# Loading a float64 weight's words into idle buffers, splitting the first key and query loads over two queues, and a newly derived order of work

## The chip, the cores and the metric

The kernel runs on one core of one Trainium2 chip. The metric is the device time of one execution in microseconds, as the median over runs. The engines named below are PE (TensorE), DVE (VectorE), ACT (ScalarE), POOL (GpSimd) and SP (SyncE, which here only issues DMAs).

## The reference

Three layers follow one another on x of 4 batches x 576 positions x 512 features.

1. Attention with 8 heads of 64: scores = q k^T / 8; in each row the 32nd largest score is the threshold, all below it are dropped, and a softmax over the rest weighs v.
2. A channel mix: xk and xr are blends of x and x shifted by one position; k = relu(xk w_k); v = (k*k) w_v; r = sigmoid(xr w_r); the result is r * v. w_k is 512 x 1024, w_v 1024 x 512, w_r 512 x 512, and all three arrive as float64.
3. A mixture of 8 experts: each token goes to one expert (the argmax of a gate, or the expert of the token before it where a local gate says so), and out = p[e] * (relu(x w1[e]) w2[e]).

## The kernel before, in words

The tokens are 18 tiles of 128. Attention goes tile by tile and, within a tile, over four pairs of heads: 72 pairs. One pair does: score matmuls (L511 for batch 0, L516 for the other batches), eviction by ACT (L498), 16 chunk maxima on DVE (MAX8, L534), candidates (L544, L547), a count (L566), a mask on POOL (L571), the threshold (L575, L578), relu on ACT (L581), subtraction on POOL (L585), exp (L589), transposes on PE (L612) and the product with v (L625). Layer 2 (`moe`, matmuls L823, L888, L916) runs for two tiles at a time beside the attention of later tiles. Then the tokens are sorted by expert and layer 3 runs.

PE takes float32 weights as a high and a low part, so `narrow` turns each 128 x 512 block of a float64 weight from pairs of 32-bit words into those two parts. There are 20 blocks, called in the order w_k (8), w_r (4), w_v (8). The steps of one block, by line: load of the raw words (L735, 512 KB); `o1` on ACT (L696); `o1b`, `o2`, `o3`, `o4` on DVE (L699, L702, L705, L708); `o4b` on ACT (L711); `hi_` on ACT (L722); a product on POOL (L719); `sum_` on PE (L725 to L727); `lo_` on ACT (L730). The raw words lie in a buffer of tag `rw` (2 buffers), the integer result of `o3` in tag `xf` (1 buffer), which `o3` takes and `sum_` and `hi_` read. The results for w_v lie in tag `wv` (8 buffers, each 128 x 2 x 512).

`Sched` sets the order before the program is built. It takes each operation with a duration, its dependencies and its buffers, plays the engines forward in a model of time, and at each free engine starts the ready operation with the lowest priority number. That number is the one in the call plus `SHIFT` of the operation's kind, plus its running index times `SLOPE`. Buffers of one tag are handed out in the order of their creation. The resulting order of start is the order in which instructions are issued; on the chip each engine takes its own list strictly in order, so an instruction that waits holds all behind it. A load in the model lands 2.3 us after its issue step ends, whatever else is under way.

`keys(b, hp)` loads the keys of two heads with four DMAs into `kn` (1 buffer), two for each head; the transposes (L391) wait for all four. `queries(t)` loads one tile of q into `qn` (1 buffer). `small` loads four small tensors (L1270 to L1273). All of these are issued on SP. `fill` puts matmuls that compute nothing (L1856) into PE's gaps in the early part of the plan.

Of the kernel before, what the change touches and what calls it, by code (L numbers as in the profile page):

```python
# [146 lines left out]
def kernel(  # L147
# [48 lines left out]
    def segs(t):  # L196
        r = []
        g = t * P
        while g < (t + 1) * P:
# [40 lines left out]
    SHIFT = {"ACT Routing.own.<lambda>": 1600.4, "ACT keys.hi": -8273.1, "ACT mix.o1": -201.7, "ACT mix.o3": -55.0,  # L240
             "ACT moe.ev": -9550.0, "ACT moe.hi": -95.1, "ACT moe.rc": 2604.1, "ACT moe.rl": -1080.6,
             "ACT moe.sig": 9217.2, "ACT moe.sq": -2233.7, "ACT narrow.hi_": -6878.4, "ACT narrow.lo_": -3354.4,
             "ACT narrow.o1": -12605.5, "ACT narrow.o4b": 7243.4, "ACT narrow.o8": 82.5, "ACT pair.<lambda>": -3944.7,
             "ACT pair.cnt": 213.0, "ACT pair.cp": 153.5, "ACT pair.ev": -1356.5, "ACT pair.ex": 943.6,
             "ACT pair.ex2": 235.0, "ACT pair.nm": 645.5, "ACT pair.rl": -2339.7, "ACT queries.hi": -1850.3,
             "ACT slots.fin": -1800.3, "ACT slots.rl": 1990.9, "ACT slots.thi": -2317.5, "ACT slots.xhi": -8276.7,
             "ACT split.hi": 4421.4, "ACT x0_t.cs": -8538.1, "ACT x0_t.ev": -41.7,
             "DVE Routing.__init__.<lambda>": -8985.9, "DVE Routing.own.<lambda>": -2828.9,
             "DVE Routing.place.<lambda>": 1634.7, "DVE Routing.place.counts": -7047.9,
             "DVE Routing.place.order": 5600.6, "DVE Routing.place.rows": 2003.5, "DVE keys.lo": -172.9,  # L250
             "DVE mix.o1": 544.4, "DVE mix.o2": -1964.2, "DVE moe.lc": -7257.5, "DVE moe.lo": 12.5,
             "DVE moe.xs": 162.4, "DVE narrow.o1b": -1351.0, "DVE narrow.o2": 483.8, "DVE narrow.o3": 375.2,
             "DVE narrow.o4": -257.8, "DVE narrow.o9": 203.0, "DVE pair.cands": 3976.7, "DVE pair.ch": -3687.6,
             "DVE pair.cn": -78.5, "DVE pair.nm": -41.5, "DVE pair.r1": -646.5, "DVE pair.rx": -109.0,
             "DVE pair.th": -290.3, "DVE queries.lo": 1224.6, "DVE slots.tlo": 1053.5, "DVE slots.xlo": -1378.6,
             "DVE split.hi": 5962.0, "DVE split.lo": -1691.1, "DVE kernel.nmu": -4805.2,
             "DVE kernel.ok_in": 1377.0,
             "DVE kernel.ok_out": -2597.9, "DVE x0_t.nrm": -3136.3,
# [6 lines left out]
             "POOL Routing.place.<lambda>": 5051.1, "POOL Routing.pool.consts_": -4153.1, "POOL mix.o1": 921.0,  # L265
             "POOL mix.o4": 110.0, "POOL moe.lo": 4123.7, "POOL moe.sq": -133.5, "POOL narrow.o5": 8398.3,
             "POOL narrow.o5r": -256.8, "POOL narrow.o6": -5082.6, "POOL narrow.o9": -14.0, "POOL pair.nbias": 3171.8,
             "POOL pair.rp": 446.6, "POOL pair.sp": -4172.9, "POOL slots.gx": 794.9, "POOL slots.sca": 6498.8,
             "POOL slots.tlo": -5777.7, "POOL split.lo": -834.2, "POOL x0_t.edge": 1874.6, "SP dma.go": 763.5,
             "SP dma.keys": 1140.5, "SP dma.kspread": 10261.3, "SP dma.qspread": -8740.8, "SP dma.queries": 686.5,  # L270
             "SP dma.raw": -11550.7, "SP dma.small": 912.7, "SP dma.vals": 3870.3, "SP load.go": -7105.4,
             "SP moe.<lambda>": -2208.6}
    SLOPE = {"ACT Routing.own.<lambda>": -861.9774, "ACT keys.hi": -45.9238, "ACT mix.o1": 16.4916,
             "ACT moe.ev": -27.2409, "ACT moe.hi": 1.4502, "ACT moe.rc": -108.553, "ACT moe.rl": 14.1884,
             "ACT moe.sig": -3.9868, "ACT moe.sq": 20.7524, "ACT narrow.hi_": 87.4735, "ACT narrow.lo_": 165.5799,
             "ACT narrow.o1": -35.4432, "ACT narrow.o4b": 78.6359, "ACT pair.<lambda>": 1.236, "ACT pair.ev": -1.9141,
             "ACT pair.ex": 2.3394, "ACT pair.rl": 0.1234, "ACT queries.hi": -79.7598, "ACT slots.fin": -42.3376,
# [1650 lines left out]
```

## Time and profile before

| | us |
|---|---|
| median of 3 runs | 1061.44 |
| lowest and highest of these | 1056.66, 1063.55 |
| the profiled execution, its own time | 1057.62 |
| its span, first to last instruction | 1055.8 |

Busy time in the span: PE 988.2, DVE 880.2, ACT 778.6, POOL 754.4. The profile is one execution; PE's busy time includes the fill matmuls. A wait is put down to what came last before the waiting instruction began.

### The profile page before, as it was taken

To read this page: it belongs to the slowest core of one execution; us is meant where nothing else is said; L and a number is where in the kernel's file an instruction comes from. 1 tells how busy PE (TensorE), PEld (TensorE's weight loads), DVE (VectorE), ACT (ScalarE), POOL (GpSimd) and SP (SyncE) were. 2 spreads that over 40 slices of the span, in tenths; PEclk is the share of its full clock that TensorE was granted. 3 is DMA by queue.
4 is the path that set the end of the run, shared out by engine and by line. 5 is a ranking of instruction groups with operands and counts; after the bars stand their busy time and mean duration, and the time that the engine had idled before them with its cause. 6 is when DMAs were issued, how large, how long until landed. Compare 5 with 4: busy or idle time off the path is not lost.

```text
span 1055.8 us, 24502 instructions
## 1 busy us (share of the span) xinstructions
PE 988.2 (94%) x7790; PEld 827.2 (78%) x7790; DVE 880.2 (83%) x3589; ACT 778.6 (74%) x1763; POOL 754.4 (71%) x858
## 2 busy tenths in 40 slices
PE   7898998899999999999999999999859999999896
PEld 6687884678787788888888788877759889888784
DVE  4998997858999999999989999958695669777672
ACT  4776786976999989989989799885335566566452
POOL 2686986666898989989978899873356757566552
PEclk9999999999999999999999999999789999999898
DMA  7421123234212353221342211003813646666650
GB/s 182 123 56 54 54 62 96 62 82 104 61 44 70 93 132 81 49 66 37 91 103 70 66 42 41 22 1 112 287 51 116 226 150 230 217 206 202 207 182 19
DMA packets 100974, 109.49 MB, mean 104 GB/s; under 512 B 49374, under 2 KB 67806, under 8 KB 100832
## 3 DMA queue, kind: packets, MB, share of 16 engines
q1 hardware_dynamic: 97312, 97.32, 32.4%
q0 software_dynamic: 3520, 10.49, 2.9%
q8 instruction: 64, 1.05, 0.4%
q14 instruction: 78, 0.64, 0.2%
HBM read 76.57 MB, written 10.49 MB: 82 GB/s over the span
## 4 chain that ended last, share of the span: by engine, by line
PE 58%; DVE 21%; ACT 8%; DMA 6%; issue 4%; SPq 0%; POOL 0%; POOLq 0%; DVEq 0%; ACTq 0%
PE pv L1808 9%; PE pb L1758 9%; PE xa L625 6%; PE pv L916 5%; PE pb L888 5%; PE pb L612 5%; DVE c L534 4%; PE pb L516 4%; PE pb L823 3%; DVE c L575 2%; PE pb L1768 2%; DVE mk L566 2%; PE pb L511 2%; PE pv L1856 2%; DMA rw<-in_moe_w_k_dram 2%
## 5 line engine op out<-in xcount | busy, mean ns | idle before, releaser
L585 POOL TENSOR_TENSOR at<-s,at 128x576 f32<-128x576 f32 x144 | 205.0, 1435 | 31.0 <-ACT at L581 30.4
L571 POOL TENSOR_TENSOR mk<-s,mk 128x576 f32<-128x576 f32 x144 | 205.6, 1428 | 0.0
L534 DVE MAX8 c<-s 128x8 f32<-128x72 f32 x1152 | 166.5, 219 | 4.8 <-ACT s L498 4.8
L581 ACT ACTIVATE at<-s,TS 128x576 f32<-128x576 f32 x144 | 112.1, 783 | 16.2 <-DVE TS L578 15.8
L1758 PE MATMUL pb<-xk,wk 128*128 128x256 f32 x864 | 114.6, 289 | 7.2 <-DVE xk L1740 7.2
L1758 PEld LDWEIGHTS pb<-xk,wk 128*128 128x128 f32 x864 | 112.3, 196 | 10.7 <-DVE xk L1740 7.5
L575 DVE MAX8 c<-mk 128x8 f32<-128x584 f32 x144 | 108.4, 757 | 14.6 <-POOL mk L571 14.6
L589 ACT ACTIVATE at<-at,sm 128x576 f32<-128x576 f32 x144 | 113.0, 786 | 7.7 <-POOL at L585 7.3
L498 ACT ACTIVATE s<-pb 128x288 f32<-128x288 f32 (+1 forms) x320 | 110.1, 418 | 8.4 <-PE pb L516 4.5
L612 PE MATMUL pb<-ident,at 128*128 128x128 f32 x648 | 99.1, 281 | 17.0 <-ACT at L589 11.8
L566 DVE TENSOR_SCALAR_CACHE_REDUCE mk<-s,c 128x576 f32<-128x576 f32 x144 | 114.8, 801 | 0.0
L615 ACT ACTIVATE aT<-pb 128x384 f32<-128x384 f32 x216 | 98.5, 497 | 12.7 <-PE pb L612 12.1
L916 PE MATMUL pv<-wv,kk 128*128 128x512 f32 x384 | 106.5, 406 | 0.0
L888 PE MATMUL pb<-xk,wk 128*128 128x256 f32 x768 | 103.9, 286 | 0.0
L612 PEld LDWEIGHTS pb<-ident,at 128*128 128x128 f32 x648 | 74.0, 142 | 37.5 <-ACT at L589 17.7
L625 PE MATMUL xa<-aT,vb 128*64 128x128 f32 (+1 forms) x1600 | 98.6, 269 | 2.4 <-ACT aT L615 1.8
L888 PEld LDWEIGHTS pb<-xk,wk 128*128 128x128 f32 x768 | 95.2, 188 | 2.9 <-issue 1.4
L625 PEld LDWEIGHTS xa<-aT,vb 128*64 128x64 f32 x1600 | 80.8, 138 | 19.2 <-issue 11.1
L1808 PE MATMUL pv<-wv,vb 128*128 128x512 f32 x330 | 88.5, 402 | 0.9 <-ACT xT L1816 0.9
L516 PE MATMUL pb<-kT,qx 128*128 128x288 f32 x480 | 86.5, 314 | 1.4 <-DMA kT<-rw 0.8
L1702 DVE TENSOR_TENSOR wk<-s,wk 128x512 fp32r<-128x512 f32 x67 | 70.7, 1088 | 16.1 <-ACT wk L1699 8.9
L516 PEld LDWEIGHTS pb<-kT,qx 128*128 128x128 f32 x480 | 69.6, 188 | 13.3 <-issue 5.3
(258 smaller groups left out, 2232.1 us busy)
## 6 DMA issues: line engine op xcount, KB each, us to landing
s<-in_moe_w_dram SPq DMA_DIRECT2D x88, 256.0 KB, 4.1
kT<-in_moe_w_dram SPq DMA_DIRECT2D x44, 512.0 KB, 5.1
qx<-qh SPq DMA_DIRECT2D x112, 64.0 KB, 2.0
qx<-ql SPq DMA_DIRECT2D x112, 64.0 KB, 2.0
kT<-rw SPq DMA_DIRECT2D x48, 144.0 KB, 2.6
xd<-rr SPq DMA_DIRECT2D x18, 256.0 KB, 2.2
rw<-in_moe_w_k_dram SPq DMA_DIRECT2D x8, 512.0 KB, 4.8
qn<-in_q_dram SPq DMA_DIRECT2D x16, 256.0 KB, 3.1
```

What stands on the lines that cost most here:

```text
L516: nc.tensor.matmul(dst(hf), qx.t[:, w, a, hp % 2, :], kt.t[:, a, c], start=(w == 0), stop=(w == 1))
L534: nc.vector.max(c8.t[:, a, c, :], s2.t[:, c * CH:(c + 1) * CH])
L566: nc.vector.tensor_scalar(mk.t[:, :S], s2.t, c8.t[:, a, NCH + 2, 7:8], 0.0, op0=OP.is_lt, op1=OP.add, accum_out=sm.t[:, 2 + a:3 + a])
L571: nc.gpsimd.tensor_tensor(mk.t[:, :S], s2.t, mk.t[:, :S], op=OP.mult)
L575: nc.vector.max(c8.t[:, a, 0, :], mk.t)
L585: nc.gpsimd.tensor_tensor(x, s2.t, x, op=OP.subtract)
L612: nc.tensor.transpose(pt.t[:, c * P:(c + 1) * P], at.t[:, (g * GB + c) * P:(g * GB + c + 1) * P], ident)
L625: nc.tensor.matmul(xa.t[a * D:(a + 1) * D, hp * P + p0:hp * P + p0 + n], vb[:, a, j, :], evs[c // GB][1].t[:, c % GB, p0:p0 + n], start=(j ...
L888: nc.tensor.matmul(pm.t[:, :N], WK[c][f // 4].t[:, x, f % 4 * P:(f % 4 + 1) * P], xk.t[:, y, c, :N], start=(m == 0), stop=(m == 3 * DC - 1))
L916: nc.tensor.matmul(pvs[ti].t, kk.t[:, x, ti * P:(ti + 1) * P], WV[f].t[:, y, :], start=(f == 0 and m == 0), stop=(f == FB - 1 and m == 2))
L1758: nc.tensor.matmul(ph.t[:, (f % 2) * N:(f % 2 + 1) * N], w[:, x], xt.t[:, y, c, :], start=(n == 0), stop=(n == 3 * DC - 1))
L1808: nc.tensor.matmul(py.t, hT.t[:, x, o_:o_ + P], w[0].t[:, y, :], start=(f == 0 and m == 0), stop=(f == FC - 1 and m == 2))
```

## The change

Raw words of w_k go to buffers of tag `wv` (`RAWK`, eight of them, created ahead of `WV`) and no longer to `rw`; w_r and w_v still use `rw`. Their load has a kind of its own, `rawk`. The model's landing time of all raw loads is 4.0 us, where it was 2.3 us. The second head's half of the very first key load, and the query load of tile 0, are issued on ACT's DMA queue; everything else stays on SP's. All of `SHIFT` and `SLOPE` have new values, and with them the whole order is derived again; the durations of the model stay.

```diff
-    SHIFT = {...  "SP dma.keys": 1140.5, "SP dma.kspread": 10261.3, "SP dma.qspread": -8740.8, "SP dma.queries": 686.5,
-             "SP dma.raw": -11550.7, "SP dma.small": 912.7, "SP dma.vals": 3870.3, ...
+    SHIFT = {...  "SP dma.keys": 934.8, "SP dma.kspread": 13318.2, "SP dma.qspread": -14480.5, "SP dma.queries": 1855.7,
+             "SP dma.raw": -14362.7, "SP dma.rawk": -223.3, "SP dma.small": 1776.8, "SP dma.vals": 1851.8,
...
-    SLOPE = {...  "SP dma.keys": 14.5103, "SP dma.raw": 27.5676, ...
+    SLOPE = {...  "SP dma.keys": 63.7004, "SP dma.raw": 10.391, "SP dma.rawk": 65.9593, ...
...
     WK = [[new("wk", [P, 2, 512], F32R) for _ in range(2)] for _ in range(DC)]
+
+    RAWK = [new("wv", [P, 2, DM]) for _ in range(2 * DC)]
     WV = [new("wv", [P, 2, DM], F32R) for _ in range(FB)]
...
         def go():
-            x, e, kk_ = kn.t, nc.sync, k[b, 2 * hp:2 * hp + 2]
+            x, kk_ = kn.t, k[b, 2 * hp:2 * hp + 2]
             for h in range(2):
+
+                e = nc.scalar if h and not (b or hp) else nc.sync
                 e.dma_start(x[:REM, :, h, :], kk_[h, :cut].rearrange("(p j) d -> p j d", j=KJ + 1))
                 e.dma_start(x[REM:, :KJ, h, :], kk_[h, cut:].rearrange("(p j) d -> p j d", j=KJ))
...
-                nc.sync.dma_start(qn.t[p0:p0 + n], q[b, :, s:s + n, :].rearrange("h p d -> p h d"))
+                (nc.sync if t else nc.scalar).dma_start(qn.t[p0:p0 + n], q[b, :, s:s + n, :].rearrange("h p d -> p h d"))
...
     def narrow(dst, split, c, f0, src, prio, lod=False):
         n = 512
-        raw = new("rw", [P, 2, S])
+        far = src is w_k
+        raw = RAWK[2 * c + f0 // n] if far else new("rw", [P, 2, S])
...
-        ld = dma([...], 1.5, prio - PAR['ra'], [raw], kind="raw")
+        ld = dma([...], 1.5, prio - PAR['ra'], [raw], kind="rawk" if far else "raw")
+        ld.lat = 4.0
```

## Rows read from the trace of the kernel before

**Rows 1.** The page: span, busy time by engine, DVE in 40 slices (tenths).

```profile
span 1055.8 us, 24502 instructions
PE 988.2 (94%) x7790; PEld 827.2 (78%) x7790; DVE 880.2 (83%) x3589; ACT 778.6 (74%) x1763; POOL 754.4 (71%) x858
DVE  4998997858999999999989999958695669777672
```

**Rows 2.** Busy time by stretch: us, then each engine (instructions), clock, DMA share, GB/s.

```profile
0.00:22.30 22.30, 16.68 (x189) 14.36 (x190) 8.15 (x20) 9.75 (x18) 4.16 (x14) 1.00 0.69 172
22.30:110.00 87.70, 80.41 (x878) 66.89 (x877) 80.63 (x357) 62.10 (x140) 62.04 (x69) 0.94 0.30 82
110.00:200.00 90.00, 82.00 (x748) 61.33 (x746) 81.20 (x355) 71.00 (x152) 71.22 (x72) 0.96 0.26 70
200.00:715.00 515.00, 499.23 (x4136) 415.42 (x4137) 470.63 (x2412) 457.36 (x1100) 436.30 (x540) 1.00 0.27 66
715.00:800.00 85.00, 69.00 (x402) 58.21 (x401) 65.48 (x214) 32.71 (x64) 33.14 (x35) 0.84 0.47 157
```

**Rows 3.** Chain that ended last, 0 to 110 us: shares by line.

```profile
by line: DMA rw<-in_moe_w_k_dram 17.3%; PE pb L511 8.4%; PE pv L1856 8.1%; DMA qn<-in_q_dram 5.3%; DVE xf L705 5.0%; DVE c L575 5.0%; DVE c L534 4.9%; PE pb L612 4.4%; DVE mk L566 4.2%; DMA rw<-in_moe_w_r_dram 3.8%; PE xa L625 3.4%; PE pb L
```

**Rows 4.** Instructions in order of time, 0 to 24 us: start, duration, engine, line.

```profile
0.75 0.89 SPq L735 DMA_DIRECT2D rw<-in_moe_w_k_dram  x2
...
4.66 0.67 ACT L696 ACTIVATE xT<-rw 128x512 f32<-128x512 f32 x1 [2.63 <-DMA rw<-in_moe_w_k_dram]
...
6.00 0.66 ACT L696 ACTIVATE xT<-rw 128x512 f32<-128x512 f32 x1 [0.67 <-DMA rw<-in_moe_w_k_dram]
...
9.32 0.67 SPq L377 DMA_DIRECT2D kn<-in_k_dram  x1
...
16.27 0.63 PE L391 MATMUL pb<-ident,kn 128*128 128x128 f32 x4 [2.39 <-DMA kn<-in_k_dram]
...
19.14 0.53 PE L511 MATMUL pb<-kT,qh 64*128 64x288 f32 x2
...
20.35 0.67 ACT L696 ACTIVATE xT<-rw 128x512 f32<-128x512 f32 x1 [2.70 <-DMA rw<-in_moe_w_k_dram]
...
21.92 1.30 ACT L498 ACTIVATE s<-pb 128x288 f32<-128x288 f32 x4
...
22.35 2.25 DVE L534 MAX8 c<-s 128x8 f32<-128x72 f32 x16 [0.21 <-ACT s L498]
```

**Rows 5.** DMA issues of 0 to 3 us: size of one, median us to landing.

```profile
rw<-in_moe_w_k_dram SPq DMA_DIRECT2D x2, 512.0 KB, 4.3
qn<-in_q_dram SPq DMA_DIRECT2D x1, 256.0 KB, 5.8
```

**Rows 6.** DMA issues of 9.2 to 12 us, the first keys, columns as above.

```profile
kn<-in_k_dram SPq DMA_DIRECT2D x2, 80.0 KB, 5.6
kn<-in_k_dram SPq DMA_DIRECT2D x2, 64.0 KB, 5.2
```

**Rows 7.** DVE from 22.3 to 200 us: count, busy us, mean ns, idle before.

```profile
L705 DVE SCALAR_TENSOR_TENSOR xf<-rw,xT 128x512 int32<-128x512 int32 x17 | 15.9, 933 | 0.5 <-PE pb L725 0.5
L702 DVE TENSOR_SCALAR xT<-xT 128x512 int32<-128x512 int32 x16 | 11.5, 718 | 0.0
L699 DVE TENSOR_SCALAR xT<-xT 128x512 f32<-128x512 f32 x16 | 9.3, 583 | 5.8 <-ACT xT L696 5.8
L708 DVE TENSOR_SCALAR xT<-xf 128x512 int32<-128x512 int32 x17 | 8.5, 500 | 0.0
```

**Rows 8.** Line L705 from 0 to 22.3 us: minimum, median, maximum ns; first, last start.

```profile
L705 DVE SCALAR_TENSOR_TENSOR xf<-rw,xT x3: 686/691/693, 7.0 to 18.8; 128x512 int32<-128x512 int32 x3
```

**Rows 9.** Line L711 on ACT, whole span: idle time before it, times, by releaser.

```profile
  DMA rw<-in_moe_w_r_dram: 4.6, 1
  DMA rw<-in_moe_w_v_dram: 2.7, 2
```

**Rows 10.** First loads of w_v, in order of time.

```profile
102.90 12.69 SPq L735 DMA_DIRECT2D rw<-in_moe_w_v_dram  x2
```

More of the change, by code (lines that the diff above doesn't have):

```diff
@@ L239 @@
              "rr": 3, "xT": 2, "sm": 13, "rw": 2, "wk": 8, "wv": 8}
[L240 to L258, printed above, removed]
[6 rows of a table removed]
[L265 to L272, printed above, removed]
@@ new lines @@
+    SLOPE = {"ACT Routing.own.<lambda>": -1348.8825, "ACT keys.hi": -32.6918, "ACT mix.o1": 16.4916,
+             "ACT moe.ev": -24.1055, "ACT moe.hi": 4.996, "ACT moe.rc": -97.8284, "ACT moe.rl": 8.4763,
+             "ACT moe.sig": 35.147, "ACT moe.sq": 11.9114, "ACT narrow.hi_": 62.5311, "ACT narrow.lo_": 196.4619,
+             "ACT narrow.o1": -13.1022, "ACT narrow.o4b": 79.0701, "ACT pair.<lambda>": -0.3891,
+             "ACT pair.ev": -2.8578, "ACT pair.ex": 4.4897, "ACT pair.rl": -1.4497, "ACT queries.hi": -84.0312,
+             "ACT slots.fin": -32.1785, "ACT slots.rl": 3.8542, "ACT slots.thi": 18.1095, "ACT slots.xhi": -30.7554,
+             "ACT split.hi": -3.9739, "ACT x0_t.cs": -87.8805, "ACT x0_t.ev": -177.7009,
+             "DVE Routing.__init__.<lambda>": -6048.9071, "DVE Routing.own.<lambda>": -77.3302,
+             "DVE Routing.place.<lambda>": -24.3395, "DVE Routing.place.counts": -288.3853,
+             "DVE Routing.place.order": 1123.455, "DVE Routing.place.rows": 9.8257, "DVE keys.lo": 4.7975,
+             "DVE mix.o1": -10.7223, "DVE mix.o2": 26.2681, "DVE moe.lc": -53.4529, "DVE moe.lo": -300.5694,
+             "DVE moe.xs": -97.1137, "DVE narrow.o1b": 77.4734, "DVE narrow.o2": -147.9401, "DVE narrow.o3": -177.0421,
+             "DVE narrow.o4": -57.5536, "DVE pair.cands": 28.5921, "DVE pair.ch": 13.933, "DVE pair.cn": 14.0394,
+             "DVE pair.rx": 1.6982, "DVE pair.th": 0.1133, "DVE queries.lo": 66.0557, "DVE slots.tlo": -12.1692,
+             "DVE slots.xlo": -47.92, "DVE split.hi": 5.0238, "DVE split.lo": -6.565,
+             "DVE kernel.nmu": -1476.3585,
+             "DVE kernel.ok_in": -3413.7394,
+             "DVE kernel.ok_out": -2168.5925, "DVE x0_t.nrm": -22.9301,
[6 rows of a table added]
+             "POOL Routing.place.<lambda>": -60.9876, "POOL Routing.pool.consts_": -55.9713, "POOL moe.lo": 42.5421,
+             "POOL narrow.o5": -1052.4322, "POOL narrow.o5r": -17.0072, "POOL narrow.o6": 200.3348,
+             "POOL pair.nbias": 10.4334, "POOL pair.rp": -1.4453, "POOL pair.sp": -0.05, "POOL slots.gx": 16.6481,
+             "POOL slots.sca": -6.6581, "POOL slots.tlo": 4.2525, "POOL split.lo": 1.2911, "POOL x0_t.edge": -21.2868,
+             "SP dma.keys": 63.7004, "SP dma.kspread": -52.5354, "SP dma.qspread": 5.0557, "SP dma.queries": -58.2705,
+             "SP dma.raw": 10.391, "SP dma.rawk": 65.9593, "SP dma.small": -89.3365, "SP dma.vals": -53.8432,
+             "SP load.go": 21.3215, "SP moe.<lambda>": -6.3229}
@@ L315 @@
              "POOL x0_t.edge": 1.17, "SP dma.keys": 1.18, "SP dma.kspread": 1.04, "SP dma.qspread": 1.12,
-             "SP dma.queries": 0.36, "SP dma.raw": 0.25, "SP dma.small": 2.05, "SP dma.vals": 1.14,
-             "SP moe.<lambda>": 0.5}
+             "SP dma.queries": 0.36, "SP dma.raw": 0.25, "SP dma.rawk": 0.25, "SP dma.small": 2.05,
+             "SP dma.vals": 1.14, "SP moe.<lambda>": 0.5}
     PORT = {"DVE narrow.o1b", "DVE narrow.o2", "DVE narrow.o3", "DVE narrow.o4", "DVE narrow.o9", "DVE split.lo", "DVE split.hi"}
@@ L734, in hl @@
             return [dst.t[:, k, :] if own else dst[:, k, c, f0:f0 + n] for k in range(2)]
[L735 removed]
+        ld = dma([lambda: nc.sync.dma_start(raw.t.rearrange("p a s -> p (a s)")[:, :2 * n].bitcast(I32), src[c * P:(c + 1) * P, 2 * f0:2 * (f0 + n)])], 1.5, prio - PAR['ra'], [raw], kind="rawk" if far else "raw")
+        ld.lat = 4.0
         o = sc_.op("ACT", 0.52, o1, [ld], prio, [nq], [raw])
```

51 lines of the change are left out of this document (26 added, 25 removed), and 24 rows, old and new, of tables (SHIFT, SLOPE).

## The prediction

> **What bounds the kernel now.** I read the page first. DVE is at 9 tenths or near it in most slices from the second on, and PE is busy for 94% of the span [rows 1]. A mean over 1055.8 us hides that they take turns, so the second view is the busy time by stretch [rows 2]. Three things are to be seen there. From 22.3 to 110 us DVE works 80.63 of 87.70 us and idles 7.1; from 110 to 200 us it idles 8.8. From 200 to 715 us PE works 499 of 515 us, and nothing shortens that stretch but less PE work or an earlier start of it. And in the first 22.3 us DVE works only 8.15 us: 14.2 us are idle, the largest hole ahead of the hand-over to layer 3 at 715 to 800 us. The change aims at the first three stretches. Whatever DVE gains before 200 us moves the PE-bound stretch forward by about as much; the most there is to gain is 14.2 + 7.1 + 8.8 = 30 us, if DVE never waited.
>
> The third view is the chain of waits over the first 110 us: loads of w_k hold 17.3% of it, 19.0 us [rows 3]. That is not the gain either, since a chain names the last of several waits, and DVE's own idle time directly behind a converted block (behind L696, which waits for the load) is 5.8 us from 22.3 to 200 us [rows 7].
>
> The fourth view is the first 24 us in order of time [rows 4]. SP issues two w_k loads; ACT uses them at 4.66 and 6.00 us. The keys are issued from 9.32 us and transposed at 16.27 us. Scores begin at 19.14 us, but ACT stands at L696 for a w_k load until 20.35 us, so they are evicted only at 21.92 us, and the first MAX8 starts at 22.35 us.
>
> **The change part by part.** All terms are against the profiled execution, 1057.6 us (its span is 1055.8 us, with 1.8 us around it). It lies 3.8 us under the median of 1061.4 us, which I add back at the end.
>
> *The order on SP.* I worked out the first priorities by hand from the numbers in the diff. For w_r's first load: -30 + 9 x 2 + 75 + 6 - 14362.7 = -14294; both `rw` buffers are free at the start, so two w_r loads go first, 1 MB that nobody needs for tens of microseconds. w_k's eight follow: -30 + 2 + 6 - 223.3 = -245 for the first, +230 for the last, all ready, all buffers free. The first keys have -100 - 5 + 934.8 = +830, and queries, small loads and values come between 1750 and 1860. So ten loads of 512 KB are ahead of SP's half of the keys.
>
> *When the first keys land.* Does a load wait for those ahead of it in its queue? The query load, issued right behind two w_k loads, took 5.8 us to land, longer than either of them although it is half the size [rows 5], so I take the queue to be in order. The spacing of the first two landings is 6.00 - 4.66 = 1.34 us for 524,288 bytes, 391 GB/s [rows 4]. (The second start could also be ACT's own pace; it had been idle 0.67 us for the load, so it was not.) The tenth lands at 4.66 + 9 x 1.34 = 16.7 us. The keys' own 288 KB and the 256 KB of queries share the same engines: 0.54 MB at 391 GB/s, 1.4 us more. The transposes need both halves, so they start near 18.1 us instead of 16.27 us: +1.9 us. Bounds: -7.7 us, if the keys didn't wait for the backlog (issue near 3.0 us, plus 5.6 us to land [rows 6], 8.6 us); +4.8 us, if the ten went at 300 GB/s (17.5 us of transfer from about 3 us on, then the keys). I take +1.9, as the same kind of load at the same place gives the rate.
>
> *The Trainium skill on the rate.* The page "DMA: Bandwidth & Descriptors", section Specifications, puts the HBM limit of one core near 358 GB/s. By that an estimate for one load is 1.46 us, the tenth would land 1.1 us later, and the forecast would be 1.1 us higher; the measured spacing disagrees, and I keep it.
>
> *ACT's wait ahead of the first eviction.* The w_k loads needed by then will have landed before the keys, since they are ahead in the queue. Of the time from transposes to MAX8 (22.35 - 16.27 = 6.1 us) ACT's wait for a load goes: eviction could start when the first three score matmuls are done, about 0.9 us after 19.14 (0.53 us for two), at 20.0 us in place of 21.92 us: -1.9 us. The first MAX8 stays where it is, near 22.4 us. Bounds 0 and -2.7 us (the whole wait at L696).
>
> *Conversions in the hole.* Before, DVE did three to three and a half blocks in the hole: L705 three times, at 7.0 to 18.8 us [rows 8]. The one `xf` buffer lets the next block's `o3` start some 5 us after the last. After the change the first w_k words land third, at 4.66 + 2 x 1.34 = 7.3 us, 2.7 us later than now. Besides, the model has the keys 2.3 us after their issue, near 8.7 us of its time, so work of the first pair goes into the lists of ACT, DVE and PE at that place, and what stands behind it waits with it until 18 us. One to three blocks fit. A block that is pushed out of the hole costs DVE 0.933 + 0.718 + 0.583 + 0.500 = 2.73 us later on [rows 7]. I take one block: +2.7 us; bounds 0 and +4.8 us (1.75 blocks).
>
> *Waits after 22.3 us.* All w_k words are there, and the model now allows 4.0 us for w_r and w_v, so other work stands ahead of a conversion whose words are under way. DVE's 5.8 us behind L696 go: -5.8 us. ACT also waits 4.6 and 2.7 us at L711 for w_r and w_v loads [rows 9]; ACT is idle for about a quarter of that time anyway, so I take -2 of these 7.3 us; bounds 0 and -7.3.
>
> *ACT's three DMA issues* cost what SP's cost, 0.67 us for a key load [rows 4], near 2 us, while ACT waits for its first words: nothing, at most +2.0 us if the first `o1` is late by as much.
>
> *The rest of the order.* Durations and work are the same, so in the PE-bound stretch I put the new numbers at 0. The view of before shows no such re-ordering; the nearest bound is the idle time that an order could win or lose in the hand-over from 715 to 800 us, 85 - 69 = 16 us of PE [rows 2]; half of it either way, -8 to +8 us.
>
> Sum: 1.9 - 1.9 + 2.7 - 5.8 - 2 + 0 = **-5.1 us**, 1052.5 us against the profiled execution, **1056 us** against the median. `wv` costs nothing: the last w_k block was through before the first w_v words were loaded, at 102.90 us [rows 10], and blocks go in turn, w_r's four between them.
>
> **The rivals.**
>
> *Faster: the keys do not wait.* If the loads are not served in order, or ACT's queue carries its part early and SP's half follows soon, keys land near 8.6 us, the first MAX8 comes 7.7 + 1.9 us earlier, and w_k is still converted in the gaps: -9.6 - 5.8 - 2 = -17.4 us, 1044 us. For it speaks a hole of 14.2 us; against it the query load's 5.8 us and the priorities. The Trainium skill speaks against it too: by the page "DMA: Bandwidth & Descriptors", section Issuing engines are not separate DMA queues, a second issuing engine saves only issue time; no row here has two queues at work, so this is open.
>
> *Slower: the backlog decides.* With the keys at 21 us (+4.8), eviction's gain kept (-1.9), 1.75 blocks pushed out (+4.8) and the lists blocked meanwhile, the first two stretches end about 8 us later, and the waits after 22.3 us are exchanged for others: +8 to +13 us, 1069 to 1075 us. It decides if the first key transposes begin after about 20 us. For it: nothing in the model knows of bandwidth, and values and small loads queue up behind as well. Against it: before, such a queue was already there, and DVE recovered.
>
> *No change: pace is set elsewhere.* `xf` paces the conversions and DVE's work is what it was; the waits removed come back as waits for `xf`. Sum near 0, 1061 us. In this case the change doesn't do what it says: w_k's early words lie idle.
>
> **How the numbers follow.** Forecast 0.54 (own range 1049 to 1063), faster rival 0.21, no change 0.11, slower rival 0.14. A difference under 1% (10.6 us) can't be told from none here. Most of the faster rival lies below 1050.8 us, with some of the forecast's lower end: 0.24. Above 1072 us lies most of the slower rival: 0.12. The rest, 0.64, is within 1%. The range takes in the faster rival's figure and the near end of the slower one: 1044 to 1069 us.
>
> **What would show it.** Two w_r loads, then eight of w_k, on SP; the first L391 near 18 us and the first MAX8 near 22 us; two blocks through `o3` by then; no wait of ACT for w_k loads after 22 us; DVE idle from 22.3 to 200 us down from 15.9 to about 8 us; the PE-bound stretch as long as before and some 5 us earlier. Wrong if the keys land before 12 us or after 20 us, or if the time changes after 200 us.

## The result and the profile after

The changed kernel takes **1074.53 us** (median of 4 runs, 1071.99 to 1075.47) against 1060.82 us for the kernel before in the same session: ratio **1.0129, interval 1.0091 to 1.0167**. Measured again beside other kernels it was 1.0127 (1.0090 to 1.0164). The profiled execution has a span of 1073.4 us, 17.6 us more than before. The forecast was 1056 us, and the range ended at 1069 us.

The page of the changed kernel, beside [rows 1]: the engines do the same work in a longer span, and DVE's first slice falls from 4 to 2 tenths.

```profile
span 1073.4 us, 24450 instructions
PE 991.4 (92%) x7773; PEld 829.9 (77%) x7773; DVE 879.2 (82%) x3589; ACT 780.7 (73%) x1763; POOL 750.4 (70%) x858
DVE  2998998767989998999989899976785668777672
```

Busy time by stretch, beside [rows 2]:

```profile
0.00:22.30 22.30, 10.11 (x118) 9.64 (x118) 3.26 (x10) 5.41 (x8) 2.06 (x8) 0.78 0.82 262
22.30:110.00 87.70, 80.28 (x893) 65.90 (x894) 79.28 (x329) 60.00 (x135) 59.66 (x67) 0.98 0.25 65
110.00:200.00 90.00, 80.25 (x709) 60.97 (x708) 85.04 (x380) 67.37 (x149) 66.88 (x72) 0.94 0.22 58
200.00:715.00 515.00, 493.69 (x4070) 411.08 (x4071) 468.89 (x2402) 455.13 (x1087) 430.48 (x514) 0.98 0.27 67
715.00:800.00 85.00, 76.00 (x472) 61.69 (x472) 57.42 (x207) 44.75 (x90) 37.34 (x63) 0.92 0.39 134
```

In the hole that the change aimed at, DVE works 3.26 us where it worked 8.15 us, while the DMA engines are busier (0.82 against 0.69). In the PE-bound stretch PE does 5.5 us less in the same 515 us; that was forecast as unchanged.

The first 29 us in order of time, beside [rows 4]:

```profile
0.74 0.89 SPq L740 DMA_DIRECT2D rw<-in_moe_w_r_dram  x2
...
1.68 8.24 SPq L740 DMA_DIRECT2D wv<-in_moe_w_k_dram  x8
...
8.49 0.66 ACT L701 ACTIVATE xT<-wv 128x512 f32<-128x512 f32 x1 [5.11 <-DMA wv<-in_moe_w_k_dram]
...
9.76 0.41 ACTq L444 DMA_DIRECT2D qn<-in_q_dram  x1
9.96 0.68 SPq L381 DMA_DIRECT2D kn<-in_k_dram  x1
...
20.34 1.09 PE L395 MATMUL pb<-ident,kn 128*128 128x128 f32 x4 [10.55 <-DMA kn<-in_k_dram]
...
21.22 1.06 PE L451 MATMUL pb<-ident,qn 128*128 128x128 f32 x4
...
23.45 2.02 PE L730 MATMUL pb<-xf,ident 128*128 128x512 f32 x2
...
26.21 0.53 PE L515 MATMUL pb<-kT,qh 64*128 64x288 f32 x2
...
28.57 2.25 DVE L538 MAX8 c<-s 128x8 f32<-128x72 f32 x16 [1.70 <-ACT s L502]
```

The order on SP is the one worked out in the prediction: two w_r loads, eight of w_k, then the keys. But the eight took SP 8.24 us to issue, 1.03 each where the first two of the program took 0.44 each; ACT's first conversion waited for its raw words until 8.49 us, and the query load stood behind it in ACT's list until 9.76 us. Keys and queries then were there at the same time, 20.3 us, and the first MAX8 began 6.2 us later than before (28.57 against 22.35).

To follow a delay further I take the start of the first MAX8 of a pair (every sixteenth instruction of that line) in each profiled execution; pairs count from 0. The first row is in us, the others are differences from it, of starts rounded to 0.1 us. Kernels called old order have the order of before (e2, e4, e7, e8); all others have the changed kernel's. Words are the raw words of a weight; paced means that their loads are issued one by one, as late as their readers allow.

| kernel | pair 0 | pair 18 | pair 36 | pair 37 | pair 71 |
|---|---|---|---|---|---|
| before | 22.4 | 238.9 | 388.0 | 398.4 | 684.8 |
| changed | +6.2 | +11.7 | +13.8 | +18.4 | +17.4 |
| changed, run again | +5.1 | +9.6 | +11.9 | +16.3 | +15.5 |
| e1 front | -3.1 | +7.6 | +9.8 | +13.9 | +13.4 |
| e2 backlog on old order | +11.6 | +11.0 | +11.0 | +11.1 | +13.5 |
| e4 queue alone, old order | -0.2 | +2.0 | +3.4 | +3.5 | +2.7 |
| e5 spread | -4.7 | +6.2 | +8.4 | +11.2 | +9.8 |
| e7 words early, old order | +0.4 | +0.6 | +2.2 | +2.3 | +3.9 |
| e8 both, old order | -3.2 | -0.2 | +1.2 | +1.3 | +1.0 |
| e9 paced, front | -1.0 | +6.6 | +11.0 | +15.5 | +16.2 |
| e10 paced | -1.5 | +8.7 | +10.9 | +15.0 | +14.3 |
| e11 without w_r | +3.7 | +13.2 | +16.1 | +18.7 | +17.2 |
| e12 other data | +6.1 | +11.5 | +14.4 | +14.9 | +14.3 |
| e13 paced, other data | -1.9 | +8.3 | +11.2 | +11.7 | +10.9 |
| e14 other data | +6.1 | +11.2 | +13.5 | +14.0 | +13.0 |
| e15 paced, other data | -1.8 | +7.9 | +12.2 | +14.3 | +13.2 |
| e16 spread early | +5.4 | +10.4 | +13.3 | +13.8 | +13.7 |
| e17 paced, spread early | -0.7 | +7.1 | +11.3 | +11.8 | +11.8 |
| e18 one load | -6.6 | +3.1 | +6.1 | +6.6 | +6.0 |

One execution stands behind each row. Two of the changed kernel differ by 1 to 2 us, so differences below that tell nothing. From pair 71 to the end the kernels with unchanged data take 366 to 373 us in these executions (371.0 before, 371.2 changed), so pair 71 stands for the end. In between, a start also depends on what the order puts between the pairs: the changed kernel is at +0.5 at pair 10, +16.6 at pair 13, -7.2 at pair 14 and +22.9 at pair 60. So pairs 0 and 71 compare the two orders, and the pairs between compare kernels of one order. Some expectations call pair 37 the 38th. The changed kernel loses 6.2 us before the first pair and 11.2 more by the last; **4.5 of these come in one step from pair 36 to pair 37**, which e12 to e17 take apart.

### The profile page after: what moved, and what is told of

The parts are those of the page before. It is cut to its first block, busy times and chain, and to the rows that moved or that the text cites. A ratio compares the mean times of both kernels' runs of the same rounds, so it can differ in the third digit from the quotient of the medians.

```text
span 1073.4 us, 24450 instructions
## 1 busy us (share of the span) xinstructions
PE 991.4 (92%) x7773; PEld 829.9 (77%) x7773; DVE 879.2 (82%) x3589; ACT 780.7 (73%) x1763; POOL 750.4 (70%) x858
## 4 chain that ended last, share of the span: by engine, by line
PE 62%; DVE 20%; ACT 8%; DMA 4%; issue 3%; POOL 2%; SPq 0%; POOLq 0%; ACTq 0%; DVEq 0%
PE pv L1814 9%; PE pb L1764 9%; PE pb L894 6%; PE xa L629 6%; PE pv L922 6%; PE pb L616 5%; PE pb L829 5%; DVE c L538 4%; PE pb L520 4%; PE pb L1774 2%; DVE mk L570 2%; DVE c L579 2%; ACT s L502 2%; ACT at L593 2%; DVE xf L710 1%
## 5 line engine op out<-in xcount | busy, mean ns | idle before, releaser
L538 DVE MAX8 c<-s 128x8 f32<-128x72 f32 x1152 | 166.5, 219 | 14.8 <-ACT s L502 14.3
L616 PE MATMUL pb<-ident,at 128*128 128x128 f32 x648 | 101.8, 282 | 23.2 <-ACT at L593 18.3
L1764 PEld LDWEIGHTS pb<-xk,wk 128*128 128x128 f32 x864 | 111.3, 195 | 12.5 <-DVE xk L1746 9.4
L579 DVE MAX8 c<-mk 128x8 f32<-128x584 f32 x144 | 108.1, 755 | 13.8 <-POOL mk L575 13.8
L619 ACT ACTIVATE aT<-pb 128x384 f32<-128x384 f32 x216 | 98.8, 498 | 12.8 <-PE pb L616 11.8
L629 PEld LDWEIGHTS xa<-aT,vb 128*64 128x64 f32 x1600 | 80.9, 139 | 19.5 <-issue 13.3
L1708 DVE TENSOR_TENSOR wk<-s,wk 128x512 fp32r<-128x512 f32 x67 | 69.3, 1067 | 13.9 <-ACT wk L1705 7.8
```

The source lines that it names most:

```text
L538: nc.vector.max(c8.t[:, a, c, :], s2.t[:, c * CH:(c + 1) * CH])
L616: nc.tensor.transpose(pt.t[:, c * P:(c + 1) * P], at.t[:, (g * GB + c) * P:(g * GB + c + 1) * P], ident)
L629: nc.tensor.matmul(xa.t[a * D:(a + 1) * D, hp * P + p0:hp * P + p0 + n], vb[:, a, j, :], evs[c // GB][1].t[:, c % GB, p0:p0 + n], start=(j ...
L1764: nc.tensor.matmul(ph.t[:, (f % 2) * N:(f % 2 + 1) * N], w[:, x], xt.t[:, y, c, :], start=(n == 0), stop=(n == 3 * DC - 1))
```

## The experiments

Theories: **(A) backlog**, ten loads ahead of the first keys cost the whole loss; **(B) order**, the newly derived order costs by itself, whatever stands in SP's list.

**e1, the first keys and queries out of the backlog.** All four key DMAs and the query load of tile 0 at the head of ACT's queue; the rest as changed.

```diff
-                e = nc.scalar if h and not (b or hp) else nc.sync
+                e = nc.sync if b or hp else nc.scalar
...
+            if not (b or hp):
+                FIRSTQ[0](nc.scalar)
```

> The changed kernel with one edit: all four DMAs of the first key load and the first query load are issued at the head of ACT's queue, ahead of anything that ACT waits for; the order of work on every engine is the changed kernel's. Theory 'backlog' (the 14 us lost come from the first keys standing behind ten 512 KB loads in SP's queue): the first key transposes start below 10 us in place of 20.34 us, the first MAX8 below 18 us in place of 28.6 us, and the time falls by 8 to 13 us, to 1062 to 1067 us. Theory 'order' (the new numbers give a worse order, w_v's blocks above all, and the start is made up for later): the first MAX8 comes as early, but the last w_v block still ends near 200 us and the time stays within 4 us of the changed kernel, 1070 to 1078 us. Rule of one shared set of DMA engines, without a second queue's own share: the keys land no earlier than half of the backlog, about 12 us, and half of the gain is seen.

Measured 1068.08 us, ratio 1.0093 (1.0062 to 1.0124). The time lies between the two expectations. First MAX8 at 19.3 us, 9.2 us earlier than in the changed kernel; at pair 71 only 4.0 of that are left. The second pair already waited again, since the second keys still stood in SP's list.

**e2, a backlog alone on the old order.** Eight loads of 512 KB that nobody reads, behind the first two of the kernel before.

```diff
+            def extra_loads():
+                for n_, x in enumerate(EXTRA):
+                    nc.sync.dma_start(x.t.rearrange("p a s -> p (a s)").bitcast(I32), w_v[n_ * P:(n_ + 1) * P, :])
```

> The kernel before with one addition: eight loads of 512 KB that nobody reads (blocks of w_v, into the eight buffers of tag wv while they are idle) on SP's queue, right behind the first two w_k loads and ahead of queries and keys; the order of work on every engine is that of before. Theory 'backlog': the first key transposes move from 16.3 to about 26 us and the time rises by as much as the first MAX8 is late, 8 to 12 us, to 1069 to 1073 us. Theory 'order': the start is made up for in the 30 us of idle time that DVE has before 200 us, and the time rises by less than 4 us, to at most 1065 us.

Measured 1072.62 us, ratio 1.0129 (1.0078 to 1.0180). On the old order the delay of the first MAX8, 11.6 us, goes through whole to the end (the span is 11.0 us longer). So (A) alone could make a loss of this size. That it gives the same ratio is chance, as the next runs show.

```profile
18.27 1.08 PE L448 MATMUL pb<-ident,qn 128*128 128x128 f32 x4 [11.72 <-DMA qn<-in_q_dram]
...
20.43 0.67 SPq L378 DMA_DIRECT2D kn<-in_k_dram  x1
...
33.99 2.25 DVE L535 MAX8 c<-s 128x8 f32<-128x72 f32 x16 [0.21 <-ACT s L499]
```

These rows of e2 show a query load landing some 10 us after its issue at 8.08 us, and SP reaching the keys only at 20.43 us.

**e3, the changed kernel with the old numbers** in `SHIFT` and `SLOPE` (w_k's kind has that of `raw`).

> The changed kernel with the SHIFT and SLOPE of before (the new kind rawk takes raw's numbers, and raw's are moved on by eight of its steps). Its plan ends 30 us later than the changed kernel's (1031.7 against 1001.9 in the model's own time), and moe's last r product starts at 722 in place of 700. Theory 'order' in its strong form, that the chip follows the plan: 1100 to 1110 us. If instead the order hardly matters and the new buffers and the backlog carry the loss: 1068 to 1080 us.

Measured 1098.28 us, ratio 1.0356 (1.0278 to 1.0433), just under the 1100 to 1110 us expected where the chip follows the plan. The numbers fit only the structure that they were derived for, so "the change without its order" can't be had by putting the old ones back.

**e4, e7, e8, parts of the change on the old order.** e4 issues the second half of the first keys and the first queries on ACT's queue, as the change does. e7 lets w_k's words go into `wv` buffers and issues each load about one block earlier, still one by one; the planner still sees the `rw` buffer (`slot`), so the order is the old one. e8 is e7 with the first keys at the head of ACT's queue and the query load ahead of the second w_k load.

```diff
# e4
+                e = nc.scalar if h and not (b or hp) else nc.sync
# e7
-        raw = new("rw", [P, 2, S])
+        slot, m = new("rw", [P, 2, S]), 2 * c + f0 // n
+        raw = RAWK[m] if far else slot
...
+            for f in FETCH[m:m + 1] if m < 2 else FETCH[m + 1:m + 2]:
+                f()
# e8, in the query step of tile 0
+            if not t:
+                FIRSTK[0](nc.scalar)
```

> The kernel before with the split over two queues alone: the second head's half of the first keys and the first queries on ACT's queue; buffers, numbers and the order of work as before. Theory 'a second queue has a share of its own': the queries land near 4 us in place of 7.5 us, and SP is free of three issues, so its keys are issued 1 to 2 us sooner; the first MAX8 is 1 to 2 us earlier and the time 0 to 2 us lower, 1058 to 1061 us. Theory 'only issue time': the queries land as late as before, 7 us, and the time is that of before within 1 us. Against both: ACT's key issues stand behind its first two waits for w_k words, at about 6.7 us, still ahead of SP's, so no loss is expected; above 1063 us would mean that ACT's issues cost the start something.

> The kernel before, order and queues unchanged, with w_k's words in the idle buffers of tag wv and each load from the third on issued about one block earlier than before (none ahead of the first keys but the one that stood there already). This is the first part of the change without its backlog and without its order. If ACT's waits for w_k words (16 us in 8 waits before) delay the first pairs: these waits fall below 6 us, the pairs 1 to 8 come 2 to 4 us earlier and the time falls by 2 to 5 us, to 1054 to 1057 us. If the waits are covered by others: 1058 to 1061 us.

> As the experiment before, and the first keys' four DMAs at the head of ACT's queue, the first queries ahead of the second w_k load on SP's. Order of before. The first key transposes near 8 us in place of 16.3 us, the first MAX8 near 17 us in place of 22.4 us; if the start passes through whole, as the backlog did, the time falls by 5 to 9 us against the kernel before, to 1050 to 1055 us. If the plan's order of the first pairs is what then holds (values, second keys), 2 to 4 us.

Measured ratios 0.9964 (0.9939 to 0.9990), 0.9973 (0.9950 to 0.9997) and 0.9969 (0.9940 to 0.9997). The structure harms nothing; each part is worth some 0.3% on the old order, and the parts don't add up. These three are faster than both kernels: e4 at 1056.53 us, below all that was expected, e7 at 1057.22 us, between its two expectations, and e8 at 1056.75 us, with the 2 to 4 us expected if the plan's order of the first pairs holds. Where their 0.3% comes from isn't shown: at pair 71 none of their profiled executions is ahead, and in e8 the 3.2 us won at pair 0 are gone by pair 18.

**e5, e9, e10, e11, the new order with fewer loads ahead of the keys.** In e5 and e9 to e11 the loads that are not issued at once are kept and issued behind a later key, value or query load. e5: loads of w_k two at a time between keys and values, w_r behind them, first keys and queries on ACT's queue. e9: one at a time, as late as their readers allow, w_r behind the queries of tile 2, front as e1. e10: as e9 with the change's own split. e11: only the two w_r loads moved back, the first eight as changed.

```diff
+        def issue(m=len(CV) - 1):
+            if m in (0, 1) or m > 9:
+                fetch()
+            else:
+                LATER[m] = fetch
```

> The changed kernel's order with no backlog at all: the first keys and queries at the head of ACT's queue as in the first experiment, and the w_k loads handed out two at a time (two at the start, two behind the small loads, two behind the second keys, two behind the first values; w_r's two first loads behind the second values). Engine order unchanged. Theory 'backlog plus order': the first MAX8 near 16 us and the second pair's near 23 us (in the first experiment 19.3 and 29.7, because the second keys still stood behind the backlog), the last w_v block ends 4 to 7 us sooner than there, near 196 us, and the time falls by a further 4 to 7 us, to 1061 to 1064 us; what is left above the kernel before, 2 to 5 us, is the new order. Theory 'order alone': no further gain, 1068 us. If backlog were all of it: 1055 us or below.

> The changed kernel's order of instructions on every engine but for where loads are issued: two w_k loads at the start, the other six one by one behind the small loads, keys and values that stand next in SP's list, the two w_r loads behind the queries of tile 2; the first keys' four DMAs and the first query load at the head of ACT's queue. So neither the first, second nor third keys have more than one or two loads ahead of them. If the backlog in the first 25 us were the whole of the loss: first MAX8 at 18 to 20 us, the 72nd pair's MAX8 (L538) within 2 us of the kernel before's 684.8 us, and 1057 to 1061 us. If the new order costs by itself (the plan's 3 us and what drifts on the chip behind it, some 5 us): first MAX8 the same, but 72nd pair 690 to 696 us, and 1062 to 1069 us. If the loss has nothing to do with the loads: 1070 us or more.

> As the kernel with paced loads and both first loads on ACT's queue, but with the change's own split: first head's keys on SP, second head's keys and the first queries on ACT's queue, the queries behind ACT's first conversions. It tells what the pacing returns without touching the split. SP now issues keys behind two loads, near 2 us, so the keys land by 9 us; the query load is still issued near 9 us but no longer beside ten loads, so it lands in 5 to 7 us (10.6 us in the changed kernel), near 16 us. First MAX8 at 20 to 23 us. If the backlog is all: 1057 to 1061 us; if the order costs by itself: 1063 to 1069 us; if the loads don't matter: 1070 us or more.

> The changed kernel without the two w_r loads at the head of SP's list (they are issued behind the queries of tile 2); the eight w_k loads stay ahead of the first keys. A dose: eight loads in place of ten. If the backlog delays by its bytes, the first key transposes and the first MAX8 come two loads' worth earlier, 2.5 to 3 us (MAX8 near 25 to 26 us in place of 28.6), ACT's first conversion starts near 5 us in place of 8.5 us, and the time is 2 to 5 us lower, 1068 to 1071 us. If only the new order or something behind 25 us sets the time: the same 1072 to 1075 us although the start is earlier.

> The changed kernel itself once more, on the chip and beside the runs of before that these experiments share: 1.009 to 1.017 of the kernel before.

Measured: e5 1.0098 (1.0061 to 1.0134), e9 1.0101 (1.0076 to 1.0127), e10 1.0094 (1.0063 to 1.0125), e11 1.0112 (1.0087 to 1.0137), the changed kernel again 1.0127. In e11 the dose comes out at the start (MAX8 at 26.1 us, 2.5 earlier), but at pair 71 it is as late as the changed kernel. Taking loads from ahead of the first keys returns 0.2 to 0.4%, with intervals that overlap with the changed kernel's, and not 1.3%: (A) in its plain form falls. e5's 1068.46 us is what was expected of the order alone, e9's 1070.62 us even what was expected if the loads don't matter; e10's 1069.28 us and e11's 1071.57 us lie between their expectations. The first MAX8 of the paced kernels comes no more than 1.5 us earlier than before, although their keys are there much earlier, and e10's rows show why:

```profile
9.86 0.61 PE L401 MATMUL pb<-ident,kn 128*128 128x128 f32 x4
...
12.83 0.66 ACT L722 ACTIVATE rr<-wv 128x512 f32<-128x512 uint32 x1 [4.21 <-DMA wv<-in_moe_w_k_dram]
...
18.61 0.67 ACT L722 ACTIVATE rr<-wv 128x512 f32<-128x512 uint32 x1 [2.96 <-DMA wv<-in_moe_w_k_dram]
...
20.91 2.25 DVE L544 MAX8 c<-s 128x8 f32<-128x72 f32 x16 [3.36 <-ACT s L508]
```

Keys are there at 9.86 us, but now ACT stands at `o4b` (L722 here) for the words of blocks that the new order converts early, and the evictions stand behind it. In the first 60 us ACT waits 13.9 us for words in e10; in the changed kernel ACT waited 5.7 us for words and PE 10.6 us for keys. Whichever goes first, the other is late.

**e12 to e15, the wait at pair 37.** In the changed kernel ACT writes the next keys into `rw`, which four DMAs to `kT` still read:

```profile
408.51 2.47 SPq L421 DMA_DIRECT2D kT<-rw  x4
...
414.75 0.60 ACT L400 ACTIVATE rw<-pb 128x512 fp32r<-128x512 f32 x1 [3.92 <-DMA kT<-rw]
```

On that line (two shapes) ACT waits 4.7 us for such DMAs in the whole span; the same line of the kernel before lists no such wait. In e12 (on the changed kernel) and e13 (on e10) the four DMAs read a w_v weight; in e14 and e15 they copy the neighbouring heads' `kT`.

> The changed kernel; the four DMAs that spread the keys of batch 2, heads 6 and 7, into kT read a w_v weight in place of the buffer rw (so these two heads' scores are other numbers; work and timing of all else are as they were). ACT's write of the next keys into rw, which waits 3.9 us near 411 us for those DMAs to land, then has nothing to wait for. If this wait is what sets the new order back by another 4 to 5 us between the 36th and the 40th pair, the first MAX8 of pair 38 comes 3 to 4 us earlier against that of pair 37 than in the changed kernel (15.0 us apart there, 10.4 us before), and the time is 2 to 4 us lower, near 1069 us. If the wait only stands in for another one behind it (PE is the bound there), the time stays at 1072 to 1075 us.

> The same edit of that one spread, in the kernel with paced loads and the change's split. Both causes together: backlog (worth 0.3 to 0.4% by the paced kernel) and this wait. If they add up: 1064 to 1067 us, ratio near 1.005 to 1.007, and what is left is the plan's own 3 us and small losses; if the wait only stands in for another: 1068 to 1070 us as without the edit.

> As the kernel that spread a w_v weight, in a form whose whole time can be compared: the four DMAs that spread the keys of batch 2, heads 6 and 7, copy the neighbouring heads' keys from their kT buffer in place of rw (these two heads are scored against the keys of heads 4 and 5). In that run pair 37 came 3.5 us earlier than in the changed kernel, and the 72nd pair and the start of layer 3 still 3.1 us earlier. If this reaches the end: 1069 to 1071 us, ratio 1.008 to 1.011. If layer 3 takes it back: 1072 to 1075 us.

> The same edit in the kernel with paced loads and the change's split. If the two causes add up to the end: 1064 to 1067 us, ratio 1.004 to 1.008. What is left above the kernel before then is the plan's 3 us and what the chip adds to it in the first 24 pairs. If not: 1068 to 1071 us.

Their whole times (2856.52, 2852.67, 1167.93 and 1163.39 us) say nothing: with a weight for keys the kernel runs its second, general computation, and with neighbouring keys layer 3 sorts other tokens and has more groups. Up to layer 3 they can be read. In e12 pair 37 is back from +18.4 to +14.9, and 3.1 us of that reach pair 71. At pair 71 e13 wins 3.4 us against e10, e14 4.4 us against the changed kernel, and e15 only 1.1 us against e10, less than two executions of one kernel can differ. The step itself is clear: from the start of pair 36 to that of pair 37 it takes 14.6 to 15.0 us with the wait (the changed kernel twice, e1, e9, e10; 13.0 and 13.2 us in e11 and e5), 10.9 us without it in e12, e13, e14, e16, e17 and e18 (12.5 in e15), and 10.5 us before.

**e16, e17, the same four DMAs earlier.** All data as they were; the spread stands right behind the key loads of batch 3, heads 2 and 3.

```diff
+            if (b, hp) == (3, 1):
+                SOON[0]()
```

> The changed kernel, all its data as they were; in SP's list the four DMAs that spread the keys of batch 2, heads 6 and 7, stand right behind the key loads of batch 3, heads 2 and 3, some 5 us ahead of their old place (behind two value loads and a query spread). They land near 409 us, before ACT's write into rw near 411 us, which waited 3.9 us for them. If the two runs with other key data were read rightly: pair 37 comes 3 to 4 us earlier, the 72nd pair and the start of layer 3 some 3 to 4.5 us earlier, and the time is 1069 to 1071 us, ratio 1.008 to 1.011 (1.0127 to 1.0129 for the changed kernel). If the value loads, now 2.5 us later, are missed instead, the gain is under 1.5 us.

> The same move in the kernel with paced loads and the change's split (ratio 1.0094 without it). If the two causes add up to the end: 1065 to 1067 us, ratio 1.005 to 1.007; the rest above the kernel before is the plan's 3 us and losses spread over the first 24 pairs. If they don't add up: 1068 to 1070 us.

e16's rows at that place:

```profile
402.61 2.48 SPq L428 DMA_DIRECT2D kT<-rw  x4
...
410.20 0.58 ACT L404 ACTIVATE rw<-pb 128x512 fp32r<-128x512 f32 x1
```

The wait is gone, and from pair 36 to 37 e16 loses 0.4 us where the changed kernel loses 4.5. Measured 1070.98 us, ratio 1.0118 (1.0086 to 1.0151), and e17 1068.28 us, 1.0084 (1.0054 to 1.0115). These ratios lie 0.08 and 0.14% above the upper ends expected, and their intervals overlap with those of the kernels without the move (1.0127 and 1.0094). e16's 1070.98 us is at the upper edge of its range, and e17's time is the one expected if the two causes don't add up. So the 4 us of the wait are shown by the trace at its place; of them 1 to 4 us are left at pair 71 in the six runs without it, and the ratios differ by 0.1%, 1 us, which can't be told from nothing.

**e18, the new order with no words to wait for.** With e16's move, and w_r's first two loads behind the queries of tile 2, all eight blocks of w_k are converted from the first load; seven are left out.

```diff
-            r = raw.t.rearrange("p a s -> p (a s)")...
+            r = (RAWK[0] if far else raw).t.rearrange("p a s -> p (a s)")...
```

> The changed kernel with the early spread, in which all eight blocks of w_k are converted from the words of the first (the other seven loads are left out, so w_k is wrong, and layer 3, which then sorts other tokens, isn't comparable); the two w_r loads stand behind the queries of tile 2. The order of instructions on ACT, DVE, PE and POOL is the changed kernel's, but nothing of it waits for words of w_k any more and no load stands ahead of keys. So it gives the new order's own price. Read at the MAX8 of pairs 0, 18, 36 and 71 against the kernel before (22.4, 238.9, 388.0, 684.8 us), which itself waits 16 us on ACT for words. If the order is sound and only its loads are late: pair 0 at 16 to 19 us, pair 18 at 234 to 241 us, pair 71 at 682 to 688 us. If the order costs by itself: pair 18 at 244 us or more, and pair 71 at 691 us or more.

The first MAX8 starts at 15.84 us, 6.5 us earlier than before, and ACT waits 1.5 us for words in 60 us, where it waited 16.0 us before. And still pair 18 is at +3.1 and pair 71 at +6.0: between the two expectations, nearer to the second. So (B) holds too: without its loads in the way the new order starts 6.5 us earlier than the old one and ends 6.0 us later. Against e18, e17's seven loads and its waits for their words cost 5.9 us at pair 0 and 5.8 us at pair 71: they delay the start, and the delay goes through. What the new order loses behind the start isn't theirs: from pair 0 to pair 18 it is 9.7 us in e18, 10.2 in e10 and 7.8 in e17. Its whole time (1152.22 us) has another layer 3 and isn't compared.

**Where the 17.4 us at pair 71 are**, by taking causes away one after the other, with one execution each: 3.7 with the wait at `rw` (changed to e16; 0.8 of it an earlier start; 1.8 against the changed kernel's second execution), 1.9 with the pacing (e17; no more than two executions of one kernel differ), 5.8 with the seven loads (e18), and 6.0 that stay, the order's own. The scheduler's own plan for the new order starts pair 71 3.0 us later than for the old (661.0 against 658.0 us of its model time) and ends 2.7 us later (1001.9 against 999.2), so about half of the 6 us is plan. What makes them up is open; two candidates, which no run tested, are in the rows of DVE.

The first is the place of w_v's blocks. Starts of `o3` from 120 us on, the eight blocks of w_v, in the kernel before, the changed kernel and e18:

```profile
L705 DVE SCALAR_TENSOR_TENSOR xf<-rw,xT x8: 649/674/1280, 126.3 to 180.4; 128x512 int32<-128x512 int32 x8
L710 DVE SCALAR_TENSOR_TENSOR xf<-rw,xT x8: 676/1290/2047, 136.0 to 193.4; 128x512 int32<-128x512 int32 x8
L725 DVE SCALAR_TENSOR_TENSOR xf<-rw,xT x8: 672/1224/1922, 124.9 to 185.6; 128x512 int32<-128x512 int32 x8
```

Between the last `o3` of w_r (103.4 us; before 114.0) and the first of w_v the changed kernel leaves 32.6 us for attention, the kernel before 12.3. The last block of w_v is 13.0 us later than before, and in e18, whose first block came 0.3 us earlier than before, still 5.2 us. The plan itself has it 6.5 us later (177.0 against 170.5 us).

The second is the duration of `o3`: for w_r and w_v it takes 1278 ns in the mean, against 933 ns [rows 7] for 17 blocks of all kinds, some 4 us over 12 blocks (some 2.5 in the changed kernel's second execution); w_k's blocks are faster than before, so it is some 3 us over all twenty.

```profile
L710 DVE SCALAR_TENSOR_TENSOR xf<-rw,xT 128x512 int32<-128x512 int32 x12 | 15.3, 1278 | 1.5 <-PE pb L730 1.3 <-DVE xT L707 0.2
L704 DVE TENSOR_SCALAR xT<-xT 128x512 f32<-128x512 f32 x18 | 12.8, 713 | 0.7 <-ACT xT L701 0.7
L710 DVE SCALAR_TENSOR_TENSOR xf<-wv,xT 128x512 int32<-128x512 int32 x7 | 4.8, 685 | 1.4 <-PE pb L730 1.4
```

These are DVE's rows from 22.3 to 200 us in the changed kernel.

## Why the prediction was wrong

- **The step that failed most is "The rest of the order", put at 0 with -8 to +8.** It measured +9 to +10 us: e10 and e17, with the loads paced and the first MAX8 no later than before, are still 1.0094 and 1.0084. Of this, 6.0 us stay at pair 71 when no words of w_k are waited for (e18); the rest is the new order's waits for words and, in e10, the wait at `rw`. The bound came from the hand-over at 715 us, but the loss is there before it: 17.4 of the span's 17.6 us at pair 71. "Durations and work are the same" doesn't make an order free: it decides when a block is converted and which late transfer holds which engine.
- **The premise, that what DVE gains or loses before 200 us moves the rest by about as much,** doesn't give the loss either: DVE's idle time up to 200 us went from 30.0 us to 19.0 + 13.4 = 32.4 us, 2.4 us more, beside a span 17.6 us longer.
- **First keys, +1.9:** measured +4.1 (20.34 against 16.27), inside the bound of +4.8. The rate was right: 412 GB/s from 10 to 12 us, against 391 assumed. Missed was the tail: keys and queries are rows of 256 bytes, moved at 226 and 111 GB/s from 17 to 19 us. The figure of the Trainium skill, "DMA: Bandwidth & Descriptors", section Specifications (near 358 GB/s for one core), is exceeded here too, by the one core that runs.
- **ACT's wait, -1.9:** it came out at +2.1. From transposes to MAX8 it took 8.2 us, not 6.1: the queries had landed no earlier than the keys, a block's `sum_` matmuls (L730 to L732) stood ahead of the scores, and PE ran at a lower clock (below). So "the first MAX8 stays where it is" failed by 6.2 us.
- **Conversions, +2.7 for one block:** two were forecast by 22.3 us; one was done, three before. The sign was right, the size off by a block and outside its bound of 1.75 blocks.
- **Waits after 22.3 us, -5.8:** right, -5.1: DVE's idle time behind a converted block is 0.7 us in the row of L704 above. ACT's waits at L711, -2 of 7.3, fell by 6.4. Neither was worth its sum: DVE's idle time from 22.3 to 200 us fell from 15.9 to 13.4 us, not to 8, since other waits took the place.
- **ACT's three issues and `wv`, 0:** nothing found against it; e4 with all of ACT's issues is 0.36% faster than before.
- **The slower rival** gave the time (1069 to 1075 us) and its point of decision (transposes after about 20 us) is met. Its mechanism explains part of it. e2 shows that a backlog passes whole to the end on the old order; on the new one, removing it returns 0.2 to 0.4%. Its chance of 0.14 was too low. One reason against that chance was in the text: nothing in the model knows of bandwidth. The 5.8 us between e17 and e18 hang on when words land; whether e18's own 6.0 us have to do with it isn't shown.

## What to carry to other kernels

A new order of work is a cost of its own: price it by the transfers that it makes early, by what stands behind each waiting instruction and by where the plan moves the blocks that later work needs, not at zero because the work is the same. When loads are brought forward, count the bytes due before the first result, and remember that a small transfer of many short rows is served by packets, not by bytes. To find where a long program lost its time, compare the start of one repeated instruction all along it, between kernels of one order or at places with the same work left, and take away causes one by one: a delay at the start may be absorbed or passed on whole, depending on the order behind it.

## What the runs showed of the hardware

**Two queues took turns by packets.** From 14 to 16 us of the changed kernel, queue q1 (SP's, rows of 4 KB) and q10 (ACT's, rows of 256 bytes): packets, MB, share.

```profile
q1 hardware_dynamic: 203, 0.73, 93.5%
q10 hardware_dynamic: 200, 0.05, 11.9%
```

One packet each, so one fifteenth of the bytes for the small one. From 17 to 18 us, when nearly all rows of 4 KB had gone and the keys (q1) stood beside the queries (q10), it was again one for one:

```profile
q1 hardware_dynamic: 399, 0.12, 66.8%
q10 hardware_dynamic: 401, 0.10, 60.8%
```

The query load was issued at 9.76 us; its first packet moved at 13.34 us, some 100 a microsecond followed up to 16 us, and most of its 1024 rows went behind that. It took 10.6 us from issue to landing, no better than the keys behind ten loads on SP's queue, with 9.9 and 9.2 us:

```profile
qn<-in_q_dram ACTq DMA_DIRECT2D x1, 256.0 KB, 10.6
kn<-in_k_dram ACTq DMA_DIRECT2D x1, 80.0 KB, 4.9
kn<-in_k_dram SPq DMA_DIRECT2D x1, 80.0 KB, 9.9
kn<-in_k_dram ACTq DMA_DIRECT2D x1, 64.0 KB, 7.2
kn<-in_k_dram SPq DMA_DIRECT2D x1, 64.0 KB, 9.2
```

The Trainium skill, "DMA: Bandwidth & Descriptors", section Queues, rings and completion order, says that each DMA engine goes round between its queues at the granularity of a packet; the trace agrees, one for one in its own count of packets, which are single rows here, where the section has some 9 to 17 descriptors to a packet. The Trainium skill's section Issuing engines are not separate DMA queues, on the same page, says that loads of several engines interleave, which agrees, and that a second one saves only issue time, on which the prediction drew; that isn't borne out: ACT's packets went beside SP's backlog and not behind it, its half of the first keys landed 4.9 and 7.2 us after issue, and in e1 keys issued on ACT's queue were transposed at 10.24 us.

It isn't always so. From 8 to 9 us in e1 nearly all packets were ACT's keys and queries, though SP was still issuing its eight loads (9.40 us from 1.68 us on); why SP's queue moved none isn't recorded:

```profile
q10 hardware_dynamic: 729, 0.18, 136.8%
q1 hardware_dynamic: 2, 0.00, 2.1%
```

**Behind its own backlog SP issues late.** Eight w_k loads took 8.24 us to issue, and after `wg_sb` at 13.34 us the next of the small loads was issued at 20.40 us; what released it isn't recorded. The second keys, at 22.61 us, could not have come much sooner: `kn` has one buffer, which PE read up to 22.58 us. In e1, where the first keys were transposed at 10.24 us, the second were issued only at 17.71 us.

**PE came back from idling at a lower clock.** Busy time by stretch in the changed kernel (PE first; clock is the third figure from the end):

```profile
1.60:9.80 8.20, 8.15 (x109) 7.98 (x109) 0.83 (x4) 1.99 (x3) 0.00 (x0) 1.00 1.00 323
9.80:20.30 10.50, 0.00 (x0) 0.00 (x0) 1.97 (x5) 2.82 (x5) 1.26 (x1) 0.63 0.92 304
20.30:28.60 8.30, 8.26 (x53) 6.04 (x54) 3.24 (x8) 4.31 (x10) 1.50 (x3) 0.65 0.46 87
```

PE did nothing for 10.5 us, and in the 8.3 us after that the granted clock was 0.65 in the mean: part of them at the lower of its two levels (1.2 and 2.4 GHz). Four key transposes took 1.09 us (0.63 before), a pair of `sum_` matmuls 2.02 us (1.08 at 28.93 us). The fill matmuls are planned by the model's time, in which the key transposes start at 8.7 us, so none was left for this gap.
